# One visit of TensorE per chunk instead of two, in a gated linear attention fused with a multiplicative feed-forward

## The chip, the cores and the metric

The kernel runs on one core of a Trainium2 chip. The metric is the device time of that core in microseconds (us). Before the change it is 499.0 us, the median of three runs (498.97 to 499.25). The profile covers one execution whose span, from the first to the last instruction, is 497.2 us.

TensorE is called PE in the profile, VectorE is DVE, ScalarE is ACT, GpSimd is POOL, SyncE is SP (here it only issues DMAs). PEld is the loading of weights into TensorE. PSUM is the memory into which TensorE writes: eight banks of 512 fp32 columns on 128 partitions.

## The reference, cut to what matters

```python
def _attn_ref(q, k, v, f_logit):            # B, H, S, D = 4, 8, 768, 48
    f = 1.0 / (1.0 + np.exp(-f_logit))
    state = np.zeros((B, H, D, D))
    for t in range(S):
        state = f[:, :, t, :, None] * state + einsum('bhd,bhe->bhde', k[:, :, t], v[:, :, t])
        y[:, :, t] = einsum('bhd,bhde->bhe', q[:, :, t], state)

def _moe_ref(x, w1, w2, w3, w_out):         # x: 3072 tokens x 384, d_ff = 1024
    return ((x @ w1) * (x @ w2) @ w3) @ w_out
```

The attention's y, rearranged to 3072 tokens by 384, is the x of the second function. The kernel folds `w3 @ w_out` into one matrix `wc` first (the weights arrive as 64-bit words and are turned into fp32 on the chip), and works on 24 chunks ("units" u = 0 .. 23) of 128 tokens, six to a sequence. Four units make a block of 512 tokens for the feed-forward.

## The kernel before: the parts that the change touches

A planner written in Python, `Plan`, is given every piece of work as a task with an engine, an assumed cost, dependencies, a priority, and the PSUM banks that it takes and frees. It fixes the order of instructions of every engine when the program is built. The engines then work through that order, each in its own stream, and wait for each other through semaphores.

The attention of one unit has five pieces on TensorE. All use fp32; a pair of heads stands on partitions 0 to 47 and 64 to 111.

```python
NF = 5                                   # PSUM banks of the feed-forward, pool "f"
# other banks: "pa" two (pairs, later the same unit's y), "pk" one
def pairs(u):                            # K^T Q, four quarters of the array: 48 rows, 64 columns
    s["pa"] = ps.tile([P, 2, NQ], F32, name="pa")
    ... nc.tensor.matmul(s["pa"][h0 : h0 + 64, par, ...], lhsT=s["K"][rows(par), ...], rhs=s["Q"][rows(par), ...])   # 16
def turn(u):                             # K by tokens, whole array
    s["pk"] = ps.tile([P, HP, R], F32, name="pk")
    ... nc.tensor.transpose(out=s["pk"][:, hp], in_=s["K"][:, hp * C : hp * C + C], identity=ident[0:R, 0:R])        # 4
def values(u):                           # masked pairs times v, two halves: 128 rows, 64 columns
    s["py"] = ps.tile([P, 2, NQ], F32, name="pa")
    ... nc.tensor.matmul(y_block(u, b)[...], lhsT=s["v"][...], rhs=s["A"][:, par, hp], ...)                         # 8
def update(u):                           # K by tokens times v, two halves
    s["pd"] = ps.tile([P, HP, R], F32, name="pk")[0:R, :, 0:D]
    ... nc.tensor.matmul(s["pd"][...], lhsT=s["kt"][...], rhs=s["v"][...])                                          # 8
def from_state(u):                       # Q times the state before, four quarters, added onto y
    ... nc.tensor.matmul(y_block(u, b)[rows(half)], lhsT=sb[(u - 1) % 2][...], rhs=s["Q"][...], start=False, ...)   # 8
```

Between them: `taken` (ACT) copies the pairs out of PSUM into A, `causal` (POOL) masks A, `turned` (ACT) copies K by tokens out, `state` (DVE) and `blocks` (ACT) make the next state, `outcome` (ACT) takes y out. A unit that opens a sequence has no `from_state`; a unit that closes one has no `turn` and no `update`. The first four units (NPE = 4) use other layouts. For the rest the tasks of TensorE are:

```python
t["a"] = plan.add("PE", 1.0, lambda: pairs(u), [t["q"], t["k"]] + past(u, 1, "y" if u > NPE else "m"), n0 - 1000, slack=0.8)
if not closes:
    t["t"] = plan.add("PE", 0.45, lambda: turn(u), [t["k"]] + past(u, 1, "d") + past(u, 2, "d"), n0 - 999, slack=0.8)
def value():
    values(u)
    if not closes:
        update(u)
    from_state(u)
t["v"] = t["s"] = plan.add("PE", ..., value, [t["c"], t["lv"]] + past(u, 0, "e") + past(u, 1, "y", "b", "d"), n0 - 998, slack=0.8)
```

So TensorE comes to the attention of a unit twice, with matrix products of the feed-forward between: once for pairs and K by tokens, once for values, update and state. `pairs(u)` waits for y of the unit before to be taken out, since both stand in the banks "pa".

The feed-forward's upward products are mostly done in a seven-product scheme, `seven(jc, which)`, on halves of 256 tokens, whose products collect in three banks X, Y, Z:

```python
pe("m1", one_, m1, [begin], 0, takes=["f"])            # X
q["k1"] = plan.add("ACT", 0.38, k1, [q["m1"]], ...)
pe("m6", one_, m6, [q["m1"]], -1, takes=["f"])         # Y
pe("m5", one_, m5, [q["m6"]], -1, takes=["f"])         # Z
dve("u2", u2, [q["k1"], q["m6"]] + old(2, "e12"))
pe("m2", two_, m2, [q["k1"], q["m5"]], -5)             # X, whose taking out c11 frees it
pe("m7", two_, m7, [q["u2"], q["m2"]], -5)             # Y
dve("u3", u3, [q["m7"]] + old(2, "e22"))
pe("m4", two_, m4, [q["u3"]], -6)                      # Y, freed by c21
pe("m3", two_, m3, [q["c22"], q["m4"]], -6)            # Z, freed by c12
```

`one_` is one matmul of 256 columns, `two_` is two. `down(i)` does the same for the products with `wc`, in pieces of four matmuls of 192 columns.

At the end of the attention, `judge` tests whether all gates lie in the range that this form of the computation allows:

```python
... seven small DVE instructions give good, one number per partition ...
count = ps.tile([P, HP, R], F32, name="pk")[0:1, 0, 0:1]
nc.tensor.matmul(count, lhsT=good, rhs=ones, start=True, stop=True)
nc.vector.tensor_scalar(left, count, R - 0.5, None, ALU.is_lt)
```

The last products of the program wait for it, and a second, general version of the whole computation follows if the test fails (here it does not run).

Of the kernel before, what the change touches and what calls it, by code (L numbers as in the profile page):

```python
# [45 lines left out]
P = 128  # L46
C = 128
# [12 lines left out]
NQ = HP * C  # L60
NPE = 4
NRAW = 3
NF = 5
DH = DM // 2
TH = TB // 2
KH = KF // 2
LOW = float.fromhex("0x1p-15")
HIGH = float.fromhex("0x1.dffffep+16")
FULL = 35.0
FLOOR = 2.0**-60  # L70
RANGE = 2.0**-40
# [134 lines left out]
def ranged(ctx, tc, q, k, f_logit, v, w1, w2, w3, w_out, out, ident, w12, wc, left):  # L206
# [21 lines left out]
    sb = [keep.tile([R, HP, R], F32, name=f"sb{i}") for i in range(2)]  # L228
    lasts = keep.tile([R, NU, HP], F32, name="lasts")
    ysum = keep.tile([R, NU], F32, name="ysum")  # L230
    ones = keep.tile([R, 1], F32, name="ones")
    warm = keep.tile([R, 1], F32, name="warm")
    perm = abp.tile([P, KH, TB], F32, name="ab").rearrange("p a b -> p (a b)")[0:R, 0 : 6 * P].rearrange("p (w c) -> p w c", c=P)

# [34 lines left out]
    def bank():  # L269

        return ps_f.tile([P, TB], F32, name=f"f{plan.got}")
# [12 lines left out]
    def setup():  # L284
        nc.scalar.activation(warm, nc.const_aps.tensor(0.0, (R, 1), F32), AF.Sigmoid)
        for i in range(2):
            nc.gpsimd.memset(fs[i][32:64], 30.0)
            nc.gpsimd.memset(ks[i][32:64], 0.0)
            nc.gpsimd.memset(qs[i][32:64], 0.0)
            if i == 0:  # L290
                make_identity(nc, ident)
        nc.gpsimd.memset(early[32:64, 2:4], 30.0)
        nc.gpsimd.memset(early[32:64, 0:2], 0.0)
        nc.gpsimd.memset(qs[2][32:64], 0.0)
        nc.gpsimd.memset(qs[3][32:64], 0.0)
        nc.vector.memset(floor, FLOOR)
        nc.vector.memset(heads(floor)[:, :, 0], 1.0)
        nc.vector.memset(back, 0.0)
        for t in gate:
            nc.vector.memset(t[:, NQ : NQ + 1], 0.0)  # L300
        nc.vector.memset(ones, 1.0)
        for t in sb:
            nc.vector.memset(t, 0.0)

        nc.gpsimd.memset(perm, 0.0)
        for i, (kc, hp) in enumerate(met):
            for par in range(2):
                for r, t, at_, n in runs(2 * hp + par):
                    if t == kc:
                        a = 64 * par + at_  # L310
                        nc.gpsimd.tensor_copy(perm[:, i, r : r + n], ident[0:R, a : a + n])
# [16 lines left out]
    def need(u):  # L328
        return (0.0, 1.0, 2.0, 3.0)[u] if u < 4 else 60 + 14.5 * (u - 4)

    def past(u, n, *names):
        return [tk[u - n][nm] for nm in names if u >= n and nm in tk[u - n]]
# [127 lines left out]
                            rhs=s["Q"][rows(par), a + 64 * late : a + C], start=True, stop=True,  # L460
                        )

    def turn(u):
        s = st[u]
        s["pk"] = ps.tile([P, HP, R], F32, name="pk")
        for hp in range(HP):
            nc.tensor.transpose(  # L467
                out=s["pk"][:, hp], in_=s["K"][:, hp * C : hp * C + C],
                identity=ident[0:R, 0:R],
            )  # L470

    def y_block(u, b):
        py = st[u]["py"]
        return py[:, b] if u < NPE else py[0:R, b // 2, b % 2 * C : b % 2 * C + C]

    def values(u):
        s = st[u]
        opens = u % NCH == 0
        if u < NPE:
            s["py"] = bank().rearrange("p (h c) -> p h c", c=C)[0:R]  # L480
        else:
            s["py"] = ps.tile([P, 2, NQ], F32, name="pa")
        met_ = set()
        for hp in heads_of(u):
            for par in range(2):
                h = 2 * hp + par
                half, b = side(u, hp, par)
                w = 64 if half == 0 else D
                zone = (half, 0 if u < NPE else par)
                nc.tensor.matmul(  # L490
                    y_block(u, b)[64 * half : 64 * half + w], lhsT=s["v"][:, h * D : h * D + w],
                    rhs=s["A"][:, par, hp], start=zone not in met_, stop=opens, skip_group_check=True,
                )
                met_.add(zone)
# [19 lines left out]

    def update(u):
        s = st[u]
        s["pd"] = ps.tile([P, HP, R], F32, name="pk")[0:R, :, 0:D]
        for hp in range(HP):
            for par in range(2):
                h = 2 * hp + par  # L520
                w = 64 if par == 0 else D
                nc.tensor.matmul(  # L522
                    s["pd"][64 * par : 64 * par + w, hp], lhsT=s["kt"][:, hp, 64 * par : 64 * par + w],
                    rhs=s["v"][:, h * D : h * D + D], start=True, stop=True,
                )

    def paired(u):
# [36 lines left out]
        if u % NCH < NCH - 1:  # L564
            def turned():
                s["kt"] = work.tile([P, HP, R], F32, name="kt")
                nc.scalar.copy(s["kt"], s["pk"])

            t["e"] = plan.add("ACT", 0.55, turned, [t["t"]] + past(u, 2, "s"), n0)

    def rest(u):
        s, t = st[u], tk[u]
# [2 lines left out]
        if u < NPE:  # L575
            t["a"] = plan.add("PE", 1.1, lambda: pairs(u), [t["q"], t["k"]] + past(u, 1, "m"), n0 - 1000)
            t["t"] = plan.add("PE", 0.45, lambda: turn(u), [t["k"]] + past(u, 1, "d"), n0 - 999)
            paired(u)
# [5 lines that stand above are left out]
            t["v"] = plan.add(  # L584
                "PE", 1.05 if opens else 2.1, value, [t["c"], t["lv"]] + past(u, 1, "b"), n0 - 998, takes=["f"],
            )
            t["s"] = plan.add("PE", 0.6, lambda: update(u), [t["e"], t["lv"]] + past(u, 1, "d"), n0 - 997)
        else:
            t["a"] = plan.add(
                "PE", 1.0, lambda: pairs(u), [t["q"], t["k"]] + past(u, 1, "y" if u > NPE else "m"), n0 - 1000, slack=0.8,  # L590
            )
            if not closes:
                t["t"] = plan.add("PE", 0.45, lambda: turn(u), [t["k"]] + past(u, 1, "d") + past(u, 2, "d"), n0 - 999, slack=0.8)
            paired(u)

            def value():
                values(u)
                if not closes:
                    update(u)
                from_state(u)  # L600

            t["v"] = t["s"] = plan.add(
                "PE", 1.2 + 0.35 * (not closes) + 0.5 * (not opens), value,
                [t["c"], t["lv"]] + past(u, 0, "e") + past(u, 1, "y", "b", "d"), n0 - 998, slack=0.8,
            )

        if not closes:
            def state():
# [9 lines left out]

            t["d"] = plan.add(
                "DVE", 0.55 if opens else 0.9, state, [t["s"], t["l"]] + [tk[u + 1][nm] for nm in "g" if nm in tk[u + 1]] + past(u, 2, "b"), n0,  # L620
                )

            def blocks():
                for par in range(2):
# [3 lines left out]

        def outcome():
            s["ys"] = work3.tile([R, HP, C], F32, name="ys")  # L630
            py = s["py"] if u < NPE else s["py"][0:R, :, 0 : 2 * C]
            ys = s["ys"]
            if u >= NPE:
                ys, py = ys.rearrange("p (b r) c -> p r b c", r=2), py.rearrange("p r (b c) -> p r b c", c=C)
            nc.scalar.activation(ys, py, AF.Copy, accum_out=ysum[:, u : u + 1])  # L635

        t["y"] = plan.add(
            "ACT", 0.8, outcome, [t["v"]] + past(u, 3, "z"),
            n0 - 10, frees=[t["v"]] if u < NPE else [],
        )  # L640

# [48 lines left out]
    def ffn(n):  # L690
# [69 lines left out]
        def seven(jc, which):  # L760
# [93 lines left out]
            pe("m6", one_, m6, [q["m1"]], -1, takes=["f"])  # L854
            pe("m5", one_, m5, [q["m6"]], -1, takes=["f"])
            dve("u2", u2, [q["k1"], q["m6"]] + old(2, "e12"))
            pe("m2", two_, m2, [q["k1"], q["m5"]], -5)
            if which == 0:
                q["c11"] = plan.add("ACT", 0.38, c11, [q["m2"]], -200, frees=[q["m1"]])
            else:  # L860
# [30 lines left out]
        def down(i):  # L891
# [59 lines left out]
            def m5():  # L951
                three(start("Z"), each(abs_[0]), each(wct[0]))

            def c22():
                q["o2"] = outs.tile([P, DM], F32, name="o")
                nc.vector.tensor_tensor(q["o2"][:, DH:DM], q["Z"], dns["u3"], ALU.add)

            def m4():
                three(q["Y"], each(quarter_(1, 1)), each(wct[3]), False)

            def c21():
                nc.vector.tensor_tensor(q["o2"][:, 0:DH], q["Y"], dns["m1"], ALU.add)

            def m3():
                three(q["Z"], each(abs_[3]), b(1, 1), False)
# [37 lines left out]
            pe("m5", m5, [q["S0"], q["m2"], q["m6"]], -3, takes=["f"])  # L1003
            dve("c22", 0.36, c22, [q["m5"], q["u3"]] + stores[-4:-2])
            pe("m4", m4, [q["u3"]], -4)
            dve("c21", 0.36, c21, [q["m4"], q["c22"]], frees=[q["m6"]])
            pe("m3", m3, [q["c22"], q["S3"], q["m4"]] + ([judged] if final else []), -4)
            dve("c12", 0.36, c12, [q["m3"], q["c11"]], frees=[q["m5"]])
            for half, deps in ((1, ("c21", "c22")), (0, ("c11", "c12"))):
# [183 lines left out]
            wc_sums.append(plan.add("DVE", 0.96, sum_down(i), folds + wc_sums[-1:], 60 + i))  # L1193


    def judge():
        low = work.tile([R, 1], F32, name="low")
        nc.vector.tensor_reduce(out=low, in_=lasts, axis=AX.XY, op=ALU.min)
# [5 lines left out]
        good = work.tile([R, 1], F32, name="good")  # L1204
        nc.vector.tensor_scalar(low, low, RANGE, None, ALU.is_ge)
        nc.vector.tensor_tensor(good, low, nil, ALU.mult)
        count = ps.tile([P, HP, R], F32, name="pk")[0:1, 0, 0:1]
        nc.tensor.matmul(count, lhsT=good, rhs=ones, start=True, stop=True)
        nc.vector.tensor_scalar(left, count, R - 0.5, None, ALU.is_lt)

    setup()
    for u in range(NU):
        front(u)
        rest(u)
        if u == NPE - 1:
            weights()
        if u == NU - 1:
            judged = plan.add("DVE", 1.5, judge, [tk[i]["y"] for i in range(NU)], -20)
        if u % UB == UB - 1:
            ffn(u // UB)  # L1220
    ready_at = 0.0
# [346 lines left out]
```

## Time and profile before

| what | value |
|---|---|
| time, median of 3 | 499.0 us |
| span of the profile | 497.2 us |
| PE busy | 484.9 us, 98% |
| DVE busy | 362.1 us, 73% |
| ACT, POOL busy | 166.8 us, 69.7 us |
| share of the span on the last chain by PE | 76% |
| DMA | 49.99 MB, 101 GB/s |

How to read it. A row of the timeline gives start, length, engine, source line, operation, tiles and shapes, and how many records were merged; the length runs to the modelled end of the last record, which overlaps what follows, so the time that a row holds TensorE is the start of the next row less its own start. An fp32 matmul leaves two records. Where several matmuls work in different parts of the array at once, their records begin almost together. In the pages of this kernel, line 457 is `pairs` in quarters, 467 `turn`, 490 `values`, 522 `update`, 509 `from_state` in quarters, 685 the feed-forward, 1143 the folding of the weights, 1208 the matmul of `judge`.

### The profile page before, as it was taken

The page shows a single profiled execution, that of the slowest core. Times are in us where ns is not written, and L with a number is a line of the kernel's source. Part 1 is how long each engine was busy: PE and PEld are TensorE (multiplying, and loading weights), DVE is VectorE, ACT ScalarE, POOL GpSimd, SP SyncE. Part 2 cuts the span into 40 slices and gives each one's busy share as a digit, 9 for nine tenths or more (in the row PEclk, how much of TensorE's full clock was granted, in tenths as well). Part 3 has the DMA queues.
Part 4 walks back from the last instruction along what each step waited for, and adds up shares of the span by engine and source line. Part 5 has one row for each costly group of instructions (what it writes and reads, how often), then busy time and mean ns, then how long its engine had stood idle before and what let it go on. Part 6 is the DMA issues. An engine that isn't in the chain of part 4 may idle for free.

```text
span 497.2 us, 9542 instructions
## 1 busy us (share of the span) xinstructions
PE 484.9 (98%) x3698; PEld 407.6 (82%) x3698; DVE 362.1 (73%) x721; ACT 166.8 (34%) x380; POOL 69.7 (14%) x115
## 2 busy tenths in 40 slices
PE   8889999999999999999999999999999999999995
PEld 6778745655799888889888888998899888889994
DVE  7998899989989677878677965446673667664541
ACT  4688456662433444443334443101100111101000
POOL 9210000432212111123212221000000000000000
PEclk9999999999999999999999999999999999999999
DMA  6889377563335554344532203100021000000011
GB/s 177 293 301 280 98 248 257 194 180 96 96 98 142 153 147 100 99 120 138 139 86 74 55 18 82 48 33 0 2 63 49 16 1 0 1 0 2 32 55 48
DMA packets 44789, 49.99 MB, mean 101 GB/s; under 512 B 15296, under 2 KB 34240, under 8 KB 43712
## 3 DMA queue, kind: packets, MB, share of 16 engines
q1 hardware_dynamic: 44736, 49.30, 33.3%
q8 instruction: 31, 0.51, 0.4%
q14 instruction: 22, 0.18, 0.1%
HBM read 40.63 MB, written 8.65 MB: 99 GB/s over the span
## 4 chain that ended last, share of the span: by engine, by line
PE 76%; POOL 1%; DVE 0%; ACT 0%; issue 0%
PE f L685 61%; PE pa L490 4%; PE f L1143 3%; PE pa L457 3%; PE pa L509 2%; PE pk L467 2%; PE pk L522 1%; POOL A L548 0%; ACT ys L635 0%; DVE place L949 0%; DVE o L970 0%; POOL A L560 0%; POOL A L559 0%; DVE nil L1202 0%; DVE zero L1200 0%
## 5 line engine op out<-in xcount | busy, mean ns | idle before, releaser
L685 PE MATMUL f<-xt,w 128*128 128x256 f32 (+1 forms) x600 | 158.5, 396 | 0.0
L685 PEld LDWEIGHTS f<-xt,w 128*128 128x128 f32 x600 | 113.6, 190 | 24.9 <-issue 11.2
L685 PE MATMUL f<-place 128*128 128x192 f32 (+1 forms) x504 | 112.6, 350 | 0.0
L685 PEld LDWEIGHTS f<-place 128*128 128x128 f32 x504 | 87.5, 190 | 6.1 <-DVE place L809 0.5
L548 POOL TENSOR_SCALAR_AFFINE_SELECT A<-A 64x256 f32<-64x256 f32 (+1 forms) x84 | 57.2, 701 | 239.2 <-PE pk L467 104.3
L1143 PE MATMUL f<-place 128*128 128x384 f32 x128 | 43.1, 490 | 0.6 <-ACT wc L1150 0.6
L788 ACT COPY a<-f 128x256 f32<-128x256 f32 x36 | 13.4, 372 | 77.4 <-PE f L685 67.2
L685 PE MATMUL f<-xt,place 128*128 128x256 f32 x144 | 37.7, 385 | 0.0
L1143 PEld LDWEIGHTS f<-place 128*128 128x128 f32 x128 | 23.8, 190 | 17.0 <-ACT wc L1150 1.2
L685 PE MATMUL f<-wc,ab 128*128 128x192 f32 x192 | 35.4, 327 | 0.0
L685 PEld LDWEIGHTS f<-wc,ab 128*128 128x128 f32 x192 | 31.9, 190 | 0.7 <-issue 0.4
L394 DVE TENSOR_TENSOR_SCAN fwd<-gate,floor 112x512 f32<-112x512 f32 x24 | 29.7, 1237 | 2.6 <-ACT gate L386 2.1
L416 DVE TENSOR_TENSOR_SCAN bwd<-gate,back 112x512 f32<-112x512 f32 x24 | 29.4, 1226 | 0.7
L812 DVE TENSOR_TENSOR place<-f,a 128x256 f32<-128x256 f32 x36 | 15.2, 423 | 20.2 <-PE f L685 20.2
L685 PEld LDWEIGHTS f<-xt,place 128*128 128x128 f32 x144 | 26.4, 189 | 4.0 <-issue 0.4
L542 ACT COPY A<-pa 64x256 f32<-64x256 f32 (+1 forms) x60 | 24.3, 439 | 13.9 <-PE pa L457 13.3
L635 ACT ACTIVATE ys<-pa 112x512 f32<-112x512 f32 x20 | 11.9, 597 | 49.9 <-PE pa L509 45.7
L490 PEld LDWEIGHTS pa<-A,vt 128*64 128x64 f32 (+1 forms) x320 | 17.6, 129 | 7.8 <-issue 5.5
L490 PE MATMUL pa<-A,vt 128*64 128x128 f32 (+1 forms) x320 | 22.7, 280 | 1.0 <-POOL A L560 1.0
L1079 ACT ACTIVATE place<-place 128x512 f32<-128x512 f32 (+2 forms) x24 | 21.2, 884 | 3.5 <-DVE w L1096 2.0
L685 PE MATMUL f<-place,w 128*128 128x256 f32 x72 | 21.6, 382 | 0.0
L1082 ACT ACTIVATE place<-place 128x512 f32<-128x512 uint32 (+2 forms) x24 | 21.1, 885 | 0.0
(117 smaller groups left out, 638.6 us busy)
## 6 DMA issues: line engine op xcount, KB each, us to landing
place<-in_w_dram SPq DMA_DIRECT2D x8, 1024.0 KB, 4.8
place<-in_w_dram SPq DMA_DIRECT2D x12, 512.0 KB, 9.3
out_dram<-o SPq DMA_DIRECT2D x24, 192.0 KB, 1.9
q<-in_q_dram SPq DMA_DIRECT2D x46, 96.0 KB, 2.4
f<-in_f_logit_dram SPq DMA_DIRECT2D x44, 96.0 KB, 2.4
k<-in_k_dram SPq DMA_DIRECT2D x44, 96.0 KB, 2.3
yt<-ys SPq DMA_DIRECT2D x40, 96.0 KB, 2.2
xt<-yt SPq DMA_DIRECT2D x20, 192.0 KB, 2.9
```

Source lines behind the costliest of these rows:

```text
L394: nc.vector.tensor_tensor_scan(s["P"], gate[u % 2][:, 0:NQ], floor, 0.0, ALU.mult, ALU.max)
L416: nc.vector.tensor_tensor_scan(s["R"][:, ::-1], gate[u % 2][:, NQ:0:-1], back[:, ::-1], 0.0, ALU.mult, ALU.max)
L457: nc.tensor.matmul(s["pa"][h0 : h0 + 64, par, a + 64 * late : a + C], lhsT=s["K"][rows(par), a + h0 : a + h0 + 64], rhs=s["Q"][rows(par), ...
L490: nc.tensor.matmul(y_block(u, b)[64 * half : 64 * half + w], lhsT=s["v"][:, h * D : h * D + w], rhs=s["A"][:, par, hp], start=zone not in ...
L542: nc.scalar.copy(parts_of(s["A"].rearrange("p r h c -> p (r h c)"))[p0:p1, :, f], parts_of(s["pa"].rearrange("p r n -> p (r n)"))[p0:p1, : ...
L548: nc.gpsimd.affine_select(out=a, in_=a, pattern=pattern, compare_op=ALU.is_ge, fill=0.0, base=0, channel_multiplier=-1,)
L685: nc.tensor.matmul(out_, lhsT=lhs[i], rhs=rhs[i], start=start and i == 0, stop=i == len(lhs) - 1, skip_group_check=True,)
L788: nc.scalar.copy(q["a"], q["X"])
L812: nc.vector.tensor_tensor(ups["u3", k], q["Y"], q["a"], ALU.add)
L1079: nc.scalar.activation(m, hi.bitcast(F32), AF.Abs)
L1082: nc.scalar.activation(lo.bitcast(F32), lo, AF.Copy, bias=2.0, scale=2.0**-51)
L1143: nc.tensor.matmul(w3s["p", jc], lhsT=w3s[jc][:, kc * P : kc * P + P], rhs=wos[:, kc], start=(kc == 0), stop=(kc == KF - 1),)
```

## The change

Its purpose: values, update and state of a unit and the pairs and K by tokens of the next unit are done in one visit of TensorE, so that TensorE changes less often between its whole array and its parts. For that the pairs of unit u + 1 must not stand in the banks of y of unit u: y gets two banks of its own, "py"; K by tokens goes into spare columns of these banks (each y takes 256 of the 512 columns of a bank); the update takes a bank of the feed-forward's pool for a short while; and the pool "f" has four banks instead of five. The range test's sum over partitions no longer uses TensorE: the 112 numbers go to DRAM and come back as one row by two DMAs, and DVE takes their minimum.

```diff
-NF = 5
+NF = 4
+LOOSE = 5
-    def turn(u):
+    def turn(u, py=None):
         s = st[u]
-        s["pk"] = ps.tile([P, HP, R], F32, name="pk")
+        s["py"] = ps.tile([P, 2, NQ], F32, name="py") if py is None else py
+        s["pk"] = s["py"][:, :, 2 * C : 2 * C + 2 * R]
...
-            s["py"] = ps.tile([P, 2, NQ], F32, name="pa")
+            s["py"] = ps.tile([P, 2, NQ], F32, name="py")
...
     def update(u):
-        s["pd"] = ps.tile([P, HP, R], F32, name="pk")[0:R, :, 0:D]
+        pd = s["py"][:, 0, 0 : 2 * C] if u < NPE else bank()
+        s["pd"] = pd[0:R, 0 : HP * D].rearrange("p (h d) -> p h d", d=D)
...
+    def together(u):
+        return u >= LOOSE
+    def begin(u):                       # pairs and turn of a unit by themselves: units 4 and 5
+        def emit():
+            pairs(u)
+            if u % NCH < NCH - 1:
+                turn(u)
...
-            t["a"] = plan.add("PE", 1.0, lambda: pairs(u), ...)
-            if not closes:
-                t["t"] = plan.add("PE", 0.45, lambda: turn(u), ...)
-            def value():
-                values(u); update(u) if not closes; from_state(u)
-            t["v"] = t["s"] = plan.add("PE", ..., value, ...)
+            more = u + 1 < NU
+            after = tk[u + 1] if more and together(u) else {}
+            def first():
+                values(u)
+                if not closes:
+                    update(u)
+            def second():
+                from_state(u)
+                if after:
+                    pairs(u + 1)
+                    if "e" in after:
+                        turn(u + 1, s["py"])
+            t["s"] = plan.add("PE", 1.1 if closes else 1.45, first,
+                [t["c"], t["lv"]] + past(u, 0, "e") + [after[nm] for nm in "qk" if after] + past(u, 1, "y", "b"), n0 - 998,
+                takes=[] if closes else ["f"], slack=0.8)
+            t["v"] = plan.add("PE", ..., second, [t["s"]], n0 - 3000)
...
             t["d"] = plan.add("DVE", ..., state, ...,
+                frees=[] if u < NPE else [t["s"]])
...
         t["y"] = plan.add(
-            "ACT", 0.8, outcome, [t["v"]] + past(u, 3, "z"),
+            "ACT", 0.8, outcome, [t["v"]] + past(u, 3, "z") + ([after["e"]] if u >= NPE and "e" in after else []),
...
-            pe("m2", two_, m2, [q["k1"], q["m5"]], -5)        # seven
+            pe("m2", two_, m2, [q["k1"], q["m6"]], -5)
...
-            dve("c21", 0.36, c21, [q["m4"], q["c22"]], frees=[q["m6"]])      # down
+            dve("c21", 0.36, c21, [q["m4"], q["c11"]] + stores[-4:-2], frees=[q["m6"]])
...
-        count = ps.tile([P, HP, R], F32, name="pk")[0:1, 0, 0:1]
-        nc.tensor.matmul(count, lhsT=good, rhs=ones, start=True, stop=True)
-        nc.vector.tensor_scalar(left, count, R - 0.5, None, ALU.is_lt)
+    def told():
+        where["all"] = dram.tile([R, 1], F32, name="good")
+        nc.sync.dma_start(where["all"], where["good"])
+    def heard():
+        row = work.tile([1, R], F32, name="row")
+        nc.sync.dma_start(row, where["all"].rearrange("r one -> one r"))
+    def decided():
+        nc.vector.tensor_reduce(out=least, in_=where["row"], axis=AX.X, op=ALU.min)
+        nc.vector.tensor_scalar(left, least, 0.5, None, ALU.is_lt)
```

No matmul other than that of the test is added or taken away, and none changes its shape. The order in which the built program lists the ranged part's matmuls for TensorE changes between array shapes (whole, halves, quarters, one column) 118 times before and 83 times after.

## The prediction

> **What bounds the kernel now.** I read the busy times by stage first, then the waits of TensorE, then the timeline of TensorE in the middle of the attention. The stages (columns: stretch, its length, PE busy and its records, PEld, DVE, ACT, POOL, clock, DMA share, GB/s):
>
> ```profile
> 36.00:140.00 104.00, 102.41 (x609) 67.23 (x608) 96.88 (x146) 57.38 (x101) 15.99 (x20) 1.00 0.57 176
> 140.00:314.00 174.00, 174.00 (x1855) 151.20 (x1853) 134.41 (x288) 69.02 (x185) 38.01 (x64) 1.00 0.39 104
> 314.00:488.90 174.90, 174.18 (x918) 160.27 (x916) 98.54 (x234) 17.91 (x50) 0.00 (x0) 1.00 0.07 22
> ```
>
> From 36 to 489 us TensorE is never short of work for long: 174.00 of 174.00 us in the stage where most of the attention is mixed with the feed-forward. There a microsecond taken from TensorE's stream is a microsecond of the end, and nothing that any other engine saves counts. TensorE's waits by releaser (total, times, longest):
>
> ```profile
> PE pa L490 <- POOL A L560: 1.0, 2, 0.7
> PE pk L467 <- DVE K L425: 1.0, 2, 0.8
> ...
> PE pk L1208 <- DVE good L1206: 0.3, 1, 0.3
> ```
>
> None of them is of the steady stage. So if the change helps, it is by what TensorE does while it counts as busy. The timeline of TensorE over one unit (start, length, line, shape, records):
>
> ```profile
> 158.98 1.47 PE L685 MATMUL f<-place,ab 128*128 128x192 f32 x8
> 160.28 1.46 PE L685 MATMUL f<-xt,w 128*128 128x256 f32 x6
> 161.67 1.13 PE L490 MATMUL pa<-A,vt 128*64 128x128 f32 x16
> 162.60 0.61 PE L522 MATMUL pk<-vt,kt 128*64 128x48 f32 x16
> 163.14 0.65 PE L509 MATMUL pa<-Q,sb 48*48 48x128 f32 x16
> 163.72 1.57 PE L685 MATMUL f<-wc,place 128*128 128x192 f32 x8
> 165.13 1.46 PE L685 MATMUL f<-xt,w 128*128 128x256 f32 x6
> 166.52 0.90 PE L457 MATMUL pa<-Q,K 48*64 48x128 f32 x32
> 167.35 0.60 PE L467 MATMUL pk<-ident,K 112*128 112x112 f32 x4
> ```
>
> The reader is to compare starts. Eight records of 192 columns followed by the same array shape hold TensorE 160.28 - 158.98 = 1.30 us, 0.1625 each, so a record of 256 columns needs 0.217 and one of 128 columns 0.108. But the six of 256 before each visit hold it 161.67 - 160.28 = 1.39 and 166.52 - 165.13 = 1.39 us, against 6 x 0.216 = 1.295. The eight records after a visit hold it 165.13 - 163.72 = 1.41 against 1.30. These differences are not work; they are the price of changing the array's shape.
>
> **What the Trainium skill says.** "TensorEngine Tiling (Array Packing)", Key Properties: "Changing tiling mode (not just tile) drains the TensorE", while tiles of one mode run at the same time. The trace agrees, with about 0.1 us on each side of a change, as above. "Perfetto Trace Analysis", Identifying the Most-Contended Engine, warns that matmul busy time says little about the distance to the peak; here too, 174.00 us of busy time hide the drains. The same page, under Matmuls, wants independent groups to rotate through banks so that taking one out overlaps the next; the trace of before has five such banks and no wait in the steady stage, and whether four suffice is the main doubt about this change. No page gives the price of a drain.
>
> **The change part by part.**
>
> *Price of a change of shape.* Whole array to quarters or halves: 0.095 us at the end of the last whole record (1.39 - 1.295), and the first wave of four is slow. The narrow timeline at `from_state` shows its second wave starting at 163.29 after 163.14, 0.15 for 0.108; at the pairs the visit lasts 167.35 - 166.52 = 0.83, where two times two waves of 128 and two of 64 columns stream in 4 x 0.108 + 4 x 0.054 = 0.65, so 0.18 for going in and out, of which I put 0.05 on the way in. Sum 0.145. Quarters to whole array: `from_state` lasts 163.72 - 163.14 = 0.58; less the first wave's 0.15 and three of 0.108 leaves 0.105 of drain; the first whole record after it is 0.11 slow (1.41 - 1.30). Sum 0.215. Halves to quarters: 0.04 for the slow first wave and, as an estimate, 0.11 of drain as in the other cases; sum 0.15. Halves to whole, estimated likewise: 0.22. From `turn` to the feed-forward there is no change (both whole).
>
> *Which changes go.* From the order of the built programs, before and after: 118 changes become 83. Whole to quarters falls from 20 to 2 (18 joined units, 5 to 22), quarters to whole from 37 to 22 (the 15 of them that have a state), halves to whole from 10 to 7 and halves to quarters rises from 17 to 20 (the 3 joined units that open a sequence: 6, 12, 18). `from_state` and the next pairs both use quarters, so I take their border as free. Turn still follows pairs, so that drain stays.
>
> - 18 x 0.145 = 2.61 us
> - 15 x 0.215 = 3.23 us
> - 3 x (0.22 - 0.15) = 0.21 us
>
> Together 6.0 us. All of these lie in the stretch in which TensorE is full.
>
> *Range test.* In the timeline the last feed-forward piece before the test's matmul starts at 314.62, the matmul at 316.48, the next piece at 316.60. Eight records need 1.30, and 0.11 of the first is the price of leaving `from_state`, which stays: 1.86 - 1.30 - 0.11 = 0.45 us lost before, 0.12 in the matmul, and 0.11 in the slow first record after it (1.57 long against 1.46 for the same eight records elsewhere). That is 0.7 us on the path, and it goes: the last products need the result only some 170 us later, so two small DMAs, whose like land in about 2 us, are hidden.
>
> *Moved, but not on the path.* The matmuls, ACT copies and POOL selects stay in number and size. DVE gets a reduce in place of a compare. Copying K by tokens out of two banks instead of one is the same 448 columns.
>
> Sum: 6.0 + 0.7 = 6.7 us; 499.0 - 6.7 = 492.3 us.
>
> **The rivals.**
>
> *Four banks starve the feed-forward.* A seven-product group holds three banks, so with four only one is spare, and for a moment in each unit the update holds one. Walked along the new order by hand, in the steady pattern after the attention: the next-but-one group's first product needs the bank that c12 frees after m3. Between m3 and it stand five matmuls of 0.432 us = 2.2 us; c12 takes 0.42 us on DVE. m5 needs the bank that c21 frees after m4; six matmuls, 2.6 us, stand between. The narrowest place is m7 of the first group of a new pair. Its u2 stands on DVE behind c12 and one multiplication; from the end of m3 I count about 0.2 us until the result can be read, then DVE starts 0.46 and 0.34 us apart (from the DVE rows at 342 us), then 0.42 us of u2 itself and a few hundredths for the signal, some 1.5 us. Four matmuls, 1.73 us, stand between. So 0.2 to 0.3 us to spare; u3 between m7 and m4 has two matmuls, 0.86 us, against about 0.65, exactly as before. It fits, but barely. Within the attention, DVE runs scans of 1.23 us in the same stream, which could push a u2 or u3 late. If each of the 36 groups lost 0.1 us, 3.6 us would be given back (about 496); at 0.2 us the gain would be gone (499 to 500). What speaks against it: the changed order already moves m5 behind m2 and interleaves the groups so that these distances exist, and DVE is 77% busy in the attention stage, 56% later.
>
> *Operands come too late for the joined visit.* Q and K of the next unit are now needed when values start, some 4.5 to 5 us earlier (166.52 against 161.67), and one late operand would hold the whole visit. In the DVE timeline K and Q for the pairs at 166.52 are both ready at 158.84, 2.8 us ahead of the values at 161.67, and the next ones at 163.77, 8.9 us ahead of the values at 172.64. Only near 151 us is a pair too late (ready at 152.14; values at 150.25), about 2 us. In return the mask on POOL, which takes 1.9 to 2.9 us after ACT's copies, gets a whole period of about 11 us. I expect at most a microsecond or two of new waits while the first joined units start, which would make it 493 to 494.
>
> *The drains hide something that has to be paid anyway*, for instance weight loads for the quarters, which the border of `from_state` and pairs would then show again. Against it: inside a visit new weights for each wave cost nothing beyond 0.108 us per wave. If true, the 0.145 of going in stays and the gain is about 4 us (495).
>
> *The early stage shifts.* Before 36 us TensorE is busy 31.4 of 36 us, and from 36 to 140 us 102.4 of 104. A different order with four banks may win or lose a microsecond there in either direction.
>
> **Range and chances.** The counted sum gives 492.3. Errors of the prices (a tenth of 6.7), the early stage (1 us either way) and possible bank waits (0 to 4 us, more likely small) make the upper side longer: 490 to 496. For faster by over 2% the time must fall under 489.0, 10 us off, which needs another 3 us from somewhere: 0.06. Slower by over 2% (over 509) would need the banks to cost 17 us: 0.02. Within 2%: 0.92.
>
> **What would show each step right or wrong.** In the changed profile the visit of a joined unit should run values, update, state, pairs and turn without a feed-forward row between, and hold TensorE about 0.93 + 0.54 + 0.47 + 0.83 + 0.43 = 3.2 us plus or minus 0.1. The pairs should start about 0.11 us after the last wave of state, not 0.22. PE busy should fall by about 6 us to 478 or 479 with its idle time little changed. The line of the range test should be gone from TensorE, with no idle near the end of the attention. If waits of TensorE for rows of the seven-product scheme (c12, c21, u2 on DVE, c11 on ACT) add up to more than 1 us, the first rival holds; if values wait for K or Q, the second. I would be wrong altogether if the feed-forward rows after 316 us, which have no attention between, took longer than before.

## The result, and the profile after the change

After the change the kernel takes 495.59 us (median of four runs, 494.95 to 496.72), against 499.08 us for the kernel before on the same chip (498.97 to 499.25). The ratio is 0.9932, with a 95% interval of 0.9913 to 0.9952. The gain is 3.5 us, inside the range that was given, and half of the 6.7 us that were added up. The profile is of the run of 496.72 us.

In the pages after the change, line 456 is `pairs`, 468 `turn`, 490 `values`, 523 `update`, 509 `from_state`, 714 the feed-forward and 978 one of its sums on DVE. Lines 1246, 1250 and 1255 are the range test's write to DRAM, its read of the row, and DVE's minimum of the row.

The joined visit is there. Rows of TensorE in the timeline of the kernel after the change, in the middle of the attention:

```profile
208.71 1.03 PE L714 MATMUL f<-xt,w 128*128 128x256 f32 x4
209.67 1.13 PE L490 MATMUL py<-A,vt 128*64 128x128 f32 x16
210.59 0.61 PE L523 MATMUL f<-vt,kt 128*64 128x48 f32 x16
211.14 0.65 PE L509 MATMUL py<-Q,sb 48*48 48x128 f32 x16
211.61 0.85 PE L456 MATMUL pa<-Q,K 48*64 48x128 f32 x32
212.39 0.60 PE L468 MATMUL py<-ident,K 112*128 112x112 f32 x4
212.83 1.48 PE L714 MATMUL f<-wc,ab 128*128 128x192 f32 x8
214.15 1.46 PE L714 MATMUL f<-place 128*128 128x192 f32 x8
```

Compare starts with those of before. The visit holds TensorE 212.83 - 209.67 = 3.16 us. `from_state` now holds it 0.47 us instead of 0.58, because the pairs after it use the same shape. The feed-forward row after `turn` holds it 1.32 us, not the 1.41 that it needs straight after the quarters. The way in costs what it did: the four records before the visit hold TensorE 209.67 - 208.71 = 0.96 us, where four of 256 columns need 0.87. What a change costs has not changed; there are fewer of them.

TensorE is as full as before in the attention, without a gap. The stages of the kernel after the change (columns as before; the counts in parentheses are records):

```profile
140.00:301.00 161.00, 161.00 (x1858) 144.53 (x1857) 127.43 (x276) 69.35 (x185) 30.72 (x64) 1.00 0.43 112
308.00:311.40 3.40, 0.22 (x2) 0.00 (x0) 0.68 (x4) 0.00 (x0) 0.00 (x0) 0.86 0.00 0
311.40:317.30 5.90, 5.90 (x18) 5.90 (x19) 1.67 (x5) 0.32 (x1) 0.00 (x0) 0.50 0.10 35
317.30:486.00 168.70, 168.70 (x873) 155.26 (x872) 95.74 (x223) 16.84 (x47) 0.00 (x0) 1.00 0.06 21
```

Two stretches stand out, right after the attention. From 308.00 to 311.40 us TensorE works 0.22 us of 3.40. In the 5.90 us after that it is busy all the time, but the column after POOL, the granted clock, is 0.50: that stretch does half the work. (The 0.86 of the stretch before is the mean of 2.45 us at full clock and 0.95 us at half, so the clock fell at about 310.45 us, while TensorE still stood idle.) TensorE's waits of the kernel after the change (total, times, longest) name the releaser:

```profile
PE f L714 <- DVE place L978: 3.6, 2, 3.2
PE f L277 <- DVE floor L297: 1.7, 1, 1.7
PE py L468 <- DVE K L424: 1.0, 2, 0.8
PE f L490 <- POOL A L549: 0.5, 1, 0.5
```

DVE's sum at line 978 is a small instruction of the feed-forward. Why it came late is seen in the timeline of all engines of the kernel after the change; brackets give the idle time before a row and its releaser:

```profile
301.65 0.16 DVE L1241 TENSOR_TENSOR good<-low,nil 112x1 f32<-112x1 f32 x1
...
301.84 0.32 SPq L1246 DMA_DIRECT2D good<-good  x1
...
306.38 0.69 DVE L950 TENSOR_TENSOR place<-place,ab 128x512 f32<-128x512 f32 x1
...
308.02 0.28 SPq L1250 DMA_DIRECT2D row<-good  x1
310.65 0.26 DVE L1255 TENSOR_REDUCE least<-row 1x1 f32<-1x112 f32 x1 [3.58 <-DMA row<-good]
310.94 0.14 DVE L1256 TENSOR_SCALAR left<-least 1x1 int32<-1x1 f32 x1
311.01 0.34 DVE L978 TENSOR_TENSOR place<-f,place 128x192 f32<-128x192 f32 x1
...
311.40 2.92 PE L714 MATMUL f<-place,ab 128*128 128x192 f32 x8 [3.19 <-DVE place L978]
```

DVE is done with line 950 at 307.07 us and then stands still for 3.58 us, because next in its order is the minimum of the row, and the row has not come back from DRAM. Line 978 stands behind it, TensorE stands behind line 978. The eight matmul records that follow last 2.92 us where others last 1.46: the half clock. The chain that ended last, of the kernel after the change (start, length, what), runs through both transfers:

```profile
301.84 6.17 DMA good<-good
308.02 2.61 DMA row<-good
```

448 bytes took 6.17 us from issue to landing. In the last 4.80 us of that the core's DMA engines moved nothing (the last two columns are their busy share and GB/s):

```profile
303.20:308.00 4.80, 4.80 (x31) 4.72 (x30) 1.74 (x3) 0.17 (x1) 0.00 (x0) 1.00 0.00 0
```

So most of the 6.17 us is not the moving of bytes, nor a queue behind other transfers; what fills it the trace does not show.

### The profile page after: what moved, and what is told of

Its sections match the earlier page's. It is cut to its first block, busy times and chain, and to the rows that moved or that the text cites. A ratio compares the mean times of both kernels' runs of the same rounds, so it can differ in the third digit from the quotient of the medians.

```text
span 495.0 us, 9560 instructions
## 1 busy us (share of the span) xinstructions
PE 481.2 (97%) x3696; PEld 411.4 (83%) x3696; DVE 360.3 (73%) x721; ACT 166.1 (34%) x380; POOL 61.6 (12%) x115
## 4 chain that ended last, share of the span: by engine, by line
PE 82%; DVE 7%; DMA 3%; issue 1%; SPq 0%; DVEq 0%
PE f L714 67%; PE f L1176 4%; PE py L490 4%; PE pa L456 2%; PE py L509 2%; PE py L468 2%; DVE place L1208 1%; DMA good<-good 1%; PE f L523 1%; DMA xt<-yt 1%; DVE place L1123 1%; DVE place L1129 1%; DVE bwd L415 1%; PE f L692 1%; DMA row<-good 1%
## 5 line engine op out<-in xcount | busy, mean ns | idle before, releaser
L549 POOL TENSOR_SCALAR_AFFINE_SELECT A<-A 64x256 f32<-64x256 f32 (+1 forms) x84 | 49.2, 606 | 231.9 <-PE py L468 105.9
L653 ACT COPY sb<-S 48x192 f32<-48x192 f32 x40 | 14.0, 350 | 27.7 <-DVE S L644 18.2
L490 PEld LDWEIGHTS py<-A,vt 128*64 128x64 f32 (+1 forms) x320 | 17.5, 129 | 6.7 <-issue 6.2
L714 PE MATMUL f<-place,ab 128*128 128x192 f32 x96 | 19.2, 346 | 3.6 <-DVE place L978 3.6
L490 PE MATMUL py<-A,vt 128*64 128x128 f32 x320 | 22.6, 281 | 0.0
```

Source lines behind the costliest of these rows:

```text
L490: nc.tensor.matmul(y_block(u, b)[64 * half : 64 * half + w], lhsT=s["v"][:, h * D : h * D + w], rhs=s["A"][:, par, hp], start=zone not in ...
L549: nc.gpsimd.affine_select(out=a, in_=a, pattern=pattern, compare_op=ALU.is_ge, fill=0.0, base=0, channel_multiplier=-1,)
L653: nc.scalar.copy(sb[u % 2][rows(par), :, 64 * par : 64 * par + D], s["S"][rows(par)])
L714: nc.tensor.matmul(out_, lhsT=lhs[i], rhs=rhs[i], start=start and i == 0, stop=i == len(lhs) - 1, skip_group_check=True,)
```

## The experiments

The theory after the result: joining the visits brings what was counted, and the range test takes most of it back, by a wait for its two transfers in the middle of DVE's stream (some 3 us) and by the half clock that the idle TensorE then gets (some 3 us). The rivals: the loss belongs to the removal of the matmul itself; four banks cost time; the joins are worth less than they look. The kernel before, run beside the first four, takes 498.92 us (median; 498.70 to 499.11), and beside the last four 498.96 us (498.39 to 499.43).

**1. The minimum later in DVE's order.** The planner is told that each of the two transfers lands 15 us later. The transfers do not change; only the places of line 1250 and of the minimum in their engines' orders do.

```diff
-            sent = moves(1, 0.4, 250, told, [looked], 0)
-            judged = plan.add("DVE", 0.2, decided, [moves(1, 0.4, 250, heard, [sent], 0)], -20)
+            sent = moves(1, 0.4, 250, told, [looked], 0, 15.0)
+            judged = plan.add("DVE", 0.2, decided, [moves(1, 0.4, 250, heard, [sent], 0, 15.0)], -20)
```

> The changed kernel, but the planner is told that each of the two small DMAs of the range test lands 15 us later than it assumed, so DVE's reduce of the row stands far later in DVE's stream; nothing else is changed. Theory A (DVE, which works in order, stands before the reduce waiting for the row, the feed-forward's next result stands behind it, TensorE idles 3.2 us and then gets half its clock for some 6 us): all of that goes, about 6 us, so 489 to 490 us, TensorE waits for L978 gone, granted clock 0.998 as before. Rival B (the shortfall lies in the four banks or in the joined visit itself): 495 us as in the changed kernel. Rival C (the wait only moves to another place in DVE's stream): DVE still waits for the row and the time lies between.

Measured: 490.29 us (490.24 to 490.47), ratio to before 0.9828 (0.9815 to 0.9842). That is 5.3 us under the changed kernel, by two assumed numbers. The write still takes 6.4 us to land. The stages of this kernel show no idle and no half clock any more:

```profile
140.00:300.00 160.00, 160.00 (x1852) 143.67 (x1852) 126.76 (x273) 68.82 (x184) 31.01 (x64) 1.00 0.42 113
300.00:480.00 180.00, 179.81 (x938) 166.01 (x936) 102.14 (x245) 18.00 (x51) 0.00 (x0) 1.00 0.07 22
```

The minimum now runs at 336.70 us, long after its row is there. This carries the theory: what was lost was lost in the wait for the row and in what followed from it.

**2. The old test in the new kernel.** The joined visits and the banks stay; the sum over partitions is a matmul with a column of ones again, as before the change, with its result in a bank of "py".

```diff
-        where["good"] = good
+        count = ps.tile([P, 2, NQ], F32, name="py")[0:1, 0, 0:1]
+        nc.tensor.matmul(count, lhsT=good, rhs=ones, start=True, stop=True)
+        nc.vector.tensor_scalar(left, count, R - 0.5, None, ALU.is_lt)
...
-            looked = plan.add("DVE", 1.0, judge, [tk[i]["y"] for i in range(NU)], -20)
-            sent = ...
-            judged = ...
+            judged = plan.add("DVE", 1.5, judge, [tk[i]["y"] for i in range(NU)], -20)
```

> The changed kernel, but with the range test's sum on TensorE as it was before the change. Theory A: no DMA in the test, so neither the wait of 3.2 us nor the half clock; the old price of the test, 0.7 us, comes back: about 490 us, 0.7 above the run with the verdict later. Rival B: 496 us. If the old test's price was hidden or was not a price, this run equals the one with the verdict later.

Measured: 491.48 us (491.24 to 491.77), ratio 0.9851 (0.9838 to 0.9865). So the matmul that the change took out was worth at most 1.2 us (against run 1), and the way in which it was taken out cost 4.1 us more than leaving it (495.59 - 491.48). Of the 1.2 us only 0.26 lies in TensorE's stream: its last row starts at 481.92 us, in run 1 at 481.66. The rest lies after the last matmul, where the two kernels have the same work. There SyncE comes to the branch that passes over the general version 0.3 us later (counted from the start of the last matmul), and its next instruction starts 3.23 us after the branch, against 2.67 us in run 1; why is open.

**3. The wait filled.** In the changed kernel eight matmuls of 256 columns, whose result nothing reads, stand in TensorE's order where it was idle. This kernel does more than the reference asks.

```diff
     def decided():
+        to = ps.tile([P, 2, NQ], F32, name="pa")[:, 0, 0:TH]
+        for _ in range(8):
+            nc.tensor.matmul(to, lhsT=floor[:, 0:P], rhs=floor[:, 0:TH], start=True, stop=True)
```

> The changed kernel with eight matmuls of 256 columns (3.5 us, their result is not used) put into TensorE's stream just where it waits for the row. The wait of DVE stays, TensorE only keeps busy during it. If the second half of the loss is the halved clock after 3.2 us of idling, the clock stays up and about 2.9 us are won: 492 to 493 us, with the granted clock at 0.998. If the halved clock has another cause, or costs nothing, the time stays at 495 to 496.

Measured: 493.69 us (493.57 to 493.85), ratio 0.9895 (0.9880 to 0.9910). The kernel with 3.46 us of useless work is 1.9 us faster than the one that waits. Rows of TensorE in its timeline, around the filling:

```profile
306.66 1.46 PE L714 MATMUL f<-wc,ab 128*128 128x192 f32 x8
307.96 3.62 PE L1256 MATMUL pa<-floor 112*128 112x256 f32 x16
311.42 1.47 PE L714 MATMUL f<-place,ab 128*128 128x192 f32 x8
312.72 1.46 PE L714 MATMUL f<-wc,place 128*128 128x192 f32 x8
```

The feed-forward resumes at the same moment as in the changed kernel (311.42 and 311.40 us), but its rows last 1.46 us at once. So the half clock is a loss of its own, and it comes from the idle stretch. The filling is 3.4 us dearer than run 1, its own length. Since both kernels resume together, their profiled runs show the price of the half clock directly: TensorE's last row starts at 485.05 us here and at 488.01 us in the changed kernel, 2.96 us later, and half of the 5.9 us at half clock is 2.95. With the 3.19 us of waiting that makes 6.1 of the 6.4 us between the profiled run of the changed kernel (496.72) and run 1. The medians give less, 1.9 us for the half clock and 5.3 us for the whole loss, because the profiled run is the slowest of the four of the changed kernel; how long the other three waited is not known.

**4. The visits apart again.** Run 1's kernel, with the constant that says from which unit on visits are joined set beyond the last unit. The built order then changes the array's shape 116 times, 33 more often than run 1.

```diff
-LOOSE = 5
+LOOSE = 24
```

> The run with the verdict later, but no unit is joined: pairs and K by tokens of every unit from 4 on stand in a visit of their own, with the change's banks (four for the feed-forward, y by itself) and its test. Prediction's own prices (0.145 into quarters, 0.215 out of them, 35 changes of shape fewer): 6.0 us slower than the joined run, so about 495 to 496. If what helped was the separate banks of y or the early stage and not the fewer changes of shape, it is within 1 us of the joined run.

Measured: 497.42 us (497.06 to 497.67), ratio 0.9969 (0.9958 to 0.9981), 7.13 us over run 1. The last row of TensorE in the timeline of run 1's kernel is

```profile
481.66 1.46 PE L714 MATMUL f<-wc,place 128*128 128x192 f32 x8
```

and in that of this one

```profile
487.85 1.46 PE L714 MATMUL f<-wc,place 128*128 128x192 f32 x8
```

so 6.19 us of the 7.13 are in TensorE's stream. The other 0.9 us are again after the last matmul, at the same place (SyncE's next instruction starts 3.30 us after the branch). TensorE does the same matmuls in both, and the prices of these 33 changes add up to 6.0 us. Up to these last rows TensorE is busy 483.26 us in run 4 and 476.20 us in run 1, so 7.06 us more, and idle 0.87 us less; the changes themselves may therefore have cost up to 7.1 us, a sixth more than counted.

**5. The kernel before with four banks.** Only the size of the feed-forward's pool changes.

```diff
-NF = 5
+NF = 4
```

> The kernel before with four banks instead of five for the feed-forward's pool and nothing else changed (pairs and y share their two banks, K by tokens keeps its own). If four banks starve the seven-product groups (0.1 to 0.2 us in each of 36), 3 to 7 us slower than before: 502 to 506, with waits of TensorE for results on DVE and ACT. If they suffice, as the slack counted in the prediction says, 498 to 500 us. If the order that the planner makes for four banks is what won the 1.8 us before 140 us, it shows here as 497 to 498.

Measured: 499.22 us (499.02 to 499.80), ratio 1.0006 (0.9999 to 1.0013). The waits of TensorE in this kernel that bear on it (total, times, longest):

```profile
PE pa L490 <- POOL A L560: 1.0, 2, 0.7
PE f L685 <- DVE place L812: 0.7, 2, 0.5
```

The second row is a wait for the seven-product scheme that before does not have, 0.7 us in two places out of 36 groups. The first, the values waiting for the last part of the mask on POOL, is in before as well. So the fifth bank was worth something, but the order that the planner makes for four banks wins about as much elsewhere: before 140 us TensorE is busy 135.07 us, in before 133.85. The time is the same within the noise, and the rival of the starved feed-forward, which asked for 3 to 7 us, falls.

**6. One more joined unit.** Run 1's kernel with one visit more joined, 81 changes of shape instead of 83.

```diff
-LOOSE = 5
+LOOSE = 4
```

> The run with the verdict later, with unit 4 joined to unit 5 as well (19 joined units instead of 18). By the prices two more changes of shape go: 0.145 + 0.215 = 0.36 us, so 489.9. If K and Q of unit 5 come too late for it (the second rival), TensorE waits for K or Q there and the time is 490.5 or more.

Measured: 490.45 us (490.32 to 490.45), ratio 0.9826 (0.9813 to 0.9840). No gain: two changes fewer are worth 0.36 us by the prices, and TensorE's last row even starts 0.11 us later than in run 1 (481.77). A wait of 0.4 us that run 1 does not have, for a copy of ACT, and 0.3 us more for the mask of POOL, show where it can have gone, while other waits moved or went. At this size the run does not settle it.

**7. The same order, wider pieces.** The changed kernel as it is, the minimum at its early place, but each of the 112 numbers is written as a row of 128 equal ones: 512 bytes in a piece instead of 4. The row is read back from the first column.

```diff
-        good = work.tile([R, 1], F32, name="good")
+        good = one.tile([R, NQ], F32, name="fwd")[:, 0:P]
-        nc.vector.tensor_tensor(good, low, nil, ALU.mult)
+        nc.vector.tensor_tensor(good, low.to_broadcast([R, P]), nil.to_broadcast([R, P]), ALU.mult)
-        where["all"] = dram.tile([R, 1], F32, name="good")
+        where["all"] = dram.tile([R, P], F32, name="good")
-        nc.sync.dma_start(row, where["all"].rearrange("r one -> one r"))
+        nc.sync.dma_start(row, where["all"][:, 0:1].rearrange("r one -> one r"))
```

> The changed kernel with its own order, but the range test's numbers are written to DRAM as 112 rows of 512 bytes instead of 112 single numbers of 4 bytes; the row read back still gathers 112 single numbers. If the 6.2 us of the first DMA come from its 4-byte pieces, it lands in 2 to 3 us, the row is there before DVE stands at its reduce, TensorE does not idle, and the time is 490 to 491. If 6 us is what any such write takes at this point, the time stays at 495 to 496.

Measured: 490.36 us (490.22 to 490.42), ratio 0.9826 (0.9811 to 0.9841), the same as run 1. The DMA issues of the changed kernel (KB, and us from issue to landing) have

```profile
good<-good SPq DMA_DIRECT2D x1, 0.4 KB, 6.2
```

and those of this kernel

```profile
good<-fwd SPq DMA_DIRECT2D x1, 56.0 KB, 1.8
row<-good SPq DMA_DIRECT2D x1, 0.4 KB, 2.1
```

128 times the bytes land in less than a third of the time. Rows of this kernel's timeline:

```profile
301.75 0.39 SPq L1246 DMA_DIRECT2D good<-fwd  x1
...
303.56 0.56 SPq L1250 DMA_DIRECT2D row<-good  x1
...
306.91 0.25 DVE L1255 TENSOR_REDUCE least<-row 1x1 f32<-1x112 f32 x1
...
307.26 0.34 DVE L978 TENSOR_TENSOR place<-f,place 128x192 f32<-128x192 f32 x1
...
307.97 1.46 PE L714 MATMUL f<-place,ab 128*128 128x192 f32 x8
```

The minimum comes without a wait, 3.7 us earlier than in the changed kernel, and TensorE goes on at full clock. So it was the length of the first transfer, and not the test's place in the order as such, that the plan could not bear; either of the two remedies is enough. Reading 112 single numbers back, each 512 bytes from the next, was not slow. "DMA: Bandwidth & Descriptors", Specifications, of the Trainium skill says that pieces below 512 bytes are read, modified and written back; that would fit a slow write, but the runs show only the times, not the mechanism: in both kernels the DMA engines stop at 303.2 us, and the landing follows 4.8 us later in the changed kernel and 0.4 us later here.

**8. The kernel before with the test by DMA alone.** As in run 1 the planner is told of a late landing; banks and visits are those of before.

```diff
-        count = ps.tile([P, HP, R], F32, name="pk")[0:1, 0, 0:1]
-        nc.tensor.matmul(count, lhsT=good, rhs=ones, start=True, stop=True)
-        nc.vector.tensor_scalar(left, count, R - 0.5, None, ALU.is_lt)
+        where["good"] = good
+    (told, heard, decided as in the change)
...
-            judged = plan.add("DVE", 1.5, judge, [tk[i]["y"] for i in range(NU)], -20)
+            (looked, sent, judged as in run 1)
```

> The kernel before with the range test by DMA alone, its verdict planned late as in the first run of this series: the change of the test by itself. The prediction's price of the test on TensorE, 0.7 us, should go: 498.2 to 498.3 us. If the test on TensorE cost nothing, no difference to the kernel before.

Measured: 498.39 us (498.12 to 498.66), ratio 0.9990 (0.9983 to 0.9996). Taking the test off TensorE is worth 0.57 us when the transfers are hidden; here the write took 7.7 us to land and cost nothing.

**The sum.** By the start of TensorE's last row, 490.33 us in before and 481.66 us in run 1, the change without its accident wins 8.67 us:

| part | from the runs | us |
|---|---|---|
| test off TensorE | before to run 8: 490.33 - 489.91 | 0.42 |
| own banks for y, four for "f", and the order that follows | run 8 to run 4: 489.91 - 487.85 | 2.06 |
| joined visits | run 4 to run 1: 487.85 - 481.66 | 6.19 |
| wait for the row, and half clock | run 1 to the changed kernel: 481.66 - 488.01 | -6.35 |

The second line is a remainder, and most of it can be placed. The stretch before 140 us in run 8, and then in run 4, is

```profile
0.00:140.00 140.00, 133.80 (x913) 93.49 (x914) 128.02 (x199) 80.02 (x146) 32.10 (x51) 1.00 0.63 197
0.00:140.00 140.00, 135.94 (x891) 96.08 (x892) 129.64 (x203) 79.00 (x145) 28.75 (x48) 1.00 0.63 197
```

so TensorE idles 2.14 us less there, before the steady attention. How that divides between the banks of y, the four banks and the new order was not separated (run 5 has 1.2 us of it with four banks alone, and loses 0.8 us between 140 and 300 us). One piece can be named: the two waits of "pa" for line 560 of POOL, 1.0 us together, which the rows of run 5 show, are in before and in runs 5 and 8; the kernels in which y has banks of its own have no wait for that line among TensorE's. Against it, run 4 waits 0.8 us for the mask of the first four units (line 549), where run 8 waits 0.3 (line 548 there).

## Why the prediction came out as it did

*The price of a change of shape* was right. The counted 6.0 us belong to 33 of the 35 changes (18 + 15 + 3 that go, 3 that come; the other two are those around the test's matmul), and these 33, put back by run 4, cost 6.19 us in TensorE's stream. The visit was to last 3.2 us plus or minus 0.1, and lasts 3.16; the pairs were to start about 0.11 us after the last wave of state, and `from_state` is 0.11 us shorter.

*Range test* is the step that failed, in its words "so two small DMAs, whose like land in about 2 us, are hidden". Two things were wrong in it. The size: the write of 112 pieces of 4 bytes took 6.17 us and the read of the row 2.61 us, 8.8 us from 301.84 to 310.65 with the gap between them. The time of 2 us came from the transfers of before, which all move 48 KB or more; that few bytes would take no longer was assumed. Run 7 shows that 2 us hold once the pieces written are wide: 1.8 us for the write, 2.1 for the read. And the kind of argument: that the last products need the result 170 us later says only that nothing waits for the *result*. The instruction that forms it waits for its *input*, at a place in DVE's order that was fixed when the program was built, and all of DVE's later work waits with it. Runs 1 and 7 remove the wait in the two possible ways and come out alike. The other half of the step, 0.7 us for the matmul that goes, was a little high: 0.57 us in the time, 0.42 us in TensorE's stream (run 8).

*The half clock* was in no step. The text did not ask what follows after TensorE has been idle for some 3 us. Here it cost as much again as the wait.

*Four banks starve the feed-forward* was rightly held unlikely: with the visits of before such waits come to 0.7 us in all (run 5), and in the changed kernel none is listed. Its 3.6 us of waiting for line 978 are in the products with `wc`, and 3.2 of them are the test's.

*Operands come too late* did not happen: no wait of values for Q or K shows among TensorE's waits; the 1.0 us of `turn` for K (line 468) is in before too. *The drains hide something* forecast 495 and so fits the time of the changed kernel by its number alone; it falls with run 4, and with `from_state`, which holds TensorE before the pairs for its four waves and no longer (0.47 us, against 0.15 + 3 x 0.108). *The early stage shifts* was put at 1 us either way; before 140 us TensorE is busy 133.85 us in before, 134.99 in run 1 and 135.94 in run 4, so it brought 1.1 to 2.1 us, the upper edge and more.

*PE busy should fall to 478 or 479* was the sign to look for; it is 481.2 us in the changed kernel, mostly because matmuls at half clock count as busy for twice as long, and 477.7 us in run 1. The sign that was set against the test, "no idle near the end of the attention", is the one that gave it away.

So 492.3 was near for a mixed reason: 2 us of gain were not foreseen, and 5.3 us of loss were not either. That 495.59 lies in the range is partly luck: the range reached up to 496 for waits for banks, which hardly came, and the test's loss took their place; one of the four runs, 496.72, lies outside. Without the loss the change brings 8.6 us by the medians (498.92 - 490.29), a ratio of 0.9828, still within 2%. Runs 1 and 7 are the fastest versions here.

## What to carry to other kernels

When work moves from a busy engine to a DMA and an idle one, ask not only who needs the result, but which instruction waits for the transfer and what stands behind it in that engine's order; give that instruction a late place, or a transfer whose landing time was measured with pieces of the same width. Price changes of the array's shape from the starts of neighbouring rows: they count as busy, no wait shows them, and 33 of them were worth 6 us. When TensorE is short of work for some 3 us, look at the granted clock of the 10 us after it before explaining the loss by the wait alone.

## What the runs showed of the hardware

The width of the pieces, and not their bytes, set the time of a small write to DRAM: 112 pieces of 4 bytes took 5.9 to 7.7 us to land (the changed kernel 6.2, runs 1, 3, 4, 6 and 8 6.4, 6.3, 5.9, 7.5 and 7.7), 112 of 512 bytes 1.8 us (run 7). In the changed kernel the DMA engines were idle for the last 4.8 of the 6.2 us; what fills that time stays open.

An idle stretch of 3.19 us on a TensorE that had been busy for 160 us without a gap brought half clock from about 310.45 to 317.28 us, some 6.8 us; with the idle stretch filled (run 3) it did not come. The clock fell 2.2 us after the modelled end of the last matmul before the gap (308.21 us), while TensorE was still idle. "TensorE: Matmul & The Clock Gate", HAM oscillation, of the Trainium skill warns of idle gaps over about 3.4 us; here one a little shorter was enough.

The changes of clock keep to a raster. In all ten traces every stretch at full clock is a whole multiple of 3.413 us long (in the changed kernel 303.79 = 89 x 3.413 before the fall, in run 1 481.28 = 141 x 3.413), and after the last matmul of the program the clock fell 2.4 us (run 4) to 5.4 us (run 6) later. So where an idle stretch lies on this raster decides how soon it costs clock; that this is why the four runs of the changed kernel differ (494.95 to 496.72) is likely, but not shown. How much of the 6.8 us is lost depends on where the idle stretch lies in it as well: in the profiled run work began again at 311.40, so 5.9 us ran at half speed.
